# Another order of reading x in the first product of most first-layer blocks

## The chip, the core and the metric

The kernel runs on one core of one Trainium2 chip. The metric is the device time of one execution in microseconds (us); below, times before are the median of three runs. The engines named are TensorE (PE for its matrix products, PEld for its weight loads), VectorE (DVE), ScalarE (ACT), GpSimd (POOL) and the DMA queue of SyncE (SP, SPq). SBUF is the memory that the engines read their operands from, PSUM the one that TensorE writes its products to.

## The reference

A banded attention over 4 batches, 8 heads, 768 positions and 64 dimensions per head, and then a two-layer network on its output:

```python
scores = scale * np.matmul(q, k.transpose(0, 1, 3, 2))
keep = is_sink | in_window           # 4 sink positions, or the last 128
scores = np.where(keep, scores, -1000000000.0)
a = softmax(scores)                  # over the last axis
attn_out = np.matmul(a, v)           # 4 x 8 x 768 x 64
x = attn_out.transpose(0, 2, 1, 3).reshape(3072, 512)
h = x @ w_in                         # 512 x 2048
g = h - np.tanh(h)
out = g @ w_out                      # 2048 x 512
```

## The kernel before

The 3072 rows of x are worked on in 12 chunks of 256 positions. For each chunk and each pair of heads the kernel computes scores (tile `s`), softmax (`p`), transposes of it (`t`, `pt`) and the product with the values, which is x of the chunk, transposed: 128 partitions by 4 parts by 256 positions. It is kept as a rounded high part `xh` and the rest, `xl`. So are the weights of both layers (`w`) and the hidden values (`gh`, `gl`): a product of two such numbers is made of three products, high by high, high by low and low by high.

The network is worked on in 96 steps: a chunk `cc` with one of 8 groups `g` of 256 hidden columns. A step `n` has three parts:

- The first-layer block (`first_half`, `mm1`): 24 products of 256 columns into the PSUM tile `h`, two halves `f` of 128 hidden columns with 12 products each (4 parts `d` of x by the three combinations). The stationary operand is a 128x128 piece of the weights, loaded anew for each product, and the moving operand is the 256 columns of `xh` or `xl` of a part. These are the products of L721. Product `k` 0 is the first of them: `xh`, part 0, first half.
- The gate (`gate`): tanh on ACT (L726), h minus it on DVE (L729), the high part on ACT (L733), the low part on DVE (L737).
- The second-layer block (`second_half`, `mm2`): 12 products of 512 columns into the PSUM tile `o` (L769), eight with `gh`, then four with `gl` as stationary operand.

The blocks and the attention are handed to a planner (`Work`) as work items with an engine, a duration, a due time and the tiles that they read and write; `Work.order` simulates the engines and gives one list, and the instructions are then issued in this order on each engine. After an `o` block `rank` prefers a ready `h` block, and a block that was begun is finished before another one is taken, where its items are ready. So PE runs `h` and `o` blocks in turns, with attention products (`s`, `t`, `x`) between them or within them; at four places two `h` blocks stand one behind the other. The gate of step n runs on ACT and DVE while PE runs the `o` block of step n - 1 and the `h` block of step n + 1.

Of the kernel before, what the change touches and what calls it, by code (L numbers as in the profile page):

```python
# [42 lines left out]
def kernel(  # L43
# [50 lines left out]
    with tc.If(bad == 0) as cmp:  # L94
        _banded(tc, qd, kp, vp, vs, masks, w_in, w_out, ident, pts, early, out)
# [79 lines left out]
        _decode_part(nc, m.bitcast(U32), lo, hi, i)  # L175


FREE = 23


class Work:
# [28 lines left out]
    def order(self):  # L210
# [14 lines left out]
        def rank(n):  # L225

            b, due = self.block[n], self.all[n][2]
            if last is None or last[1] < FREE or self.all[n][0] != "PE":
                return (1, due, n)
# [33 lines left out]
def _banded(tc, qd, kp, vp, vs, masks, w_in, w_out, ident, pts, early, out):  # L263
    nc = tc.nc
    et = mybir.EngineType
    with ExitStack() as ctx:

        def pool(name, bufs, **kw):
            return ctx.enter_context(tc.tile_pool(name=name, bufs=bufs, **kw))
# [7 lines left out]
        spool, pp, sm = pool("spool", 1), pool("pp", 2), pool("sm", 4)  # L277
        ps_s, ps_t, ps_x = pool("ps_s", 1, space=PSUM), pool("ps_t", 1, space=PSUM), pool("ps_x", 1, space=PSUM)
        ps_h, ps_o = pool("ps_h", 2, space=PSUM), pool("ps_o", 1, space=PSUM)
        work = Work()  # L280


        RAW, TWO, CUT, DUO, PB, ZL, TK = 12, 12, 1, 3, 4, 0, 1100
# [427 lines left out]
        hps, gr, gh, gl, ops, ob = ({} for _ in range(6))  # L711

        def mm1(n, k):
            cc, g = order[n]
            if k == 0:
                hps[n] = ps_h.tile([P, 2, CH], F32, tag="h", name=f"h{n}")
            f, r = divmod(k, 12)
            d, t = divmod(r, 3)
            w = wt[0, g][:, (0, 0, 1)[t], d, f * P : (f + 1) * P]
            x = (xh, xl, xh)[t][cc][:, d, :]  # L720
            nc.tensor.matmul(hps[n][:, f, :], lhsT=w, rhs=x, start=r == 0, stop=r == 11)  # L721

        def gate(n):
            def tanh():
# [63 lines left out]
        def first_half(n):  # L788
            cc, g = order[n]
            for f in range(2):  # L790
                for z in range(2):
                    def some(k0=f * 12 + z * 6):
                        for k in range(k0, k0 + 6):
                            mm1(n, k)

                    x = [("xu", home(cc), 2 * z), ("xu", home(cc), 2 * z + 1), ("x", home(cc))]
                    work.add("PE", 722, due_step(n), some, x + [("w", 0, g)], [("h", n % 2)], block=("h", n))
# [67 lines left out]
        second_half(NS - 1)  # L865

        todo, _ = work.order()
        with tc.manual_schedule(engines={et.PE, et.SP, et.DVE, et.Activation, et.Pool}):
            for n in todo:
                work.all[n][3]()  # L870
# [204 lines left out]
```

## Time and profile before

| | us |
|---|---|
| median of three runs | 686.13 (685.95 to 686.75) |
| the profiled execution | 685.93 |
| its span, first to last instruction | 684.2 |
| PE busy in it | 670.8 (98%), 4604 products |
| DVE busy | 426.7 (62%) |
| ACT busy | 368.0 (54%) |

The span is what the trace covers; the execution's own time is 1.7 us longer. A product's record in the trace runs from its start to the modelled end of its last result, some 280 ns for 256 columns, and the records of products that follow each other overlap. How fast PE works is read from the distance between two starts. [...]

### The profile page before, as it was taken

What the parts mean: (1) busy time and instruction counts of PE and PEld (TensorE: products, weight loads), DVE (VectorE), ACT (ScalarE), POOL (GpSimd) and SP (SyncE); (2) the same over time, 40 slices, a digit from 0 to 9 for tenths busy, and PEclk for the clock granted to TensorE, in tenths of its full rate; (3) what the DMA queues carried; (4) which work ended last, traced back from release to release, by engine and by line L of the source; (5) the groups of instructions that cost most, each with busy time, mean ns of one, the idle gap of its engine ahead of it and who ended that gap; (6) DMA issues with size and microseconds to landing.
All of it is one profiled execution on the core that took longest, in us unless ns stands there. A gap on an engine that the chain in (4) does not pass through costs nothing.

```text
span 684.2 us, 12421 instructions
## 1 busy us (share of the span) xinstructions
PE 670.8 (98%) x4604; PEld 599.9 (88%) x4604; DVE 426.7 (62%) x1084; ACT 368.0 (54%) x1001; POOL 50.8 (7%) x201
## 2 busy tenths in 40 slices
PE   7999999999999999999999999999999999999997
PEld 5777899999989989989989998998998998998996
DVE  6889999937945656556655665565555656564221
ACT  5996433347835564465455655555556456553222
POOL 6220000000000010000001000001000000000000
PEclk9999999999999999999999999999999999999999
DMA  6789800022221122112103102012103101100001
GB/s 200 249 265 386 327 1 5 0 70 75 55 90 29 28 97 67 28 59 74 41 28 109 54 30 89 29 54 91 28 29 101 42 28 59 59 1 1 32 1 35
DMA packets 31713, 52.13 MB, mean 76 GB/s; under 512 B 3229, under 2 KB 21021, under 8 KB 31645
## 3 DMA queue, kind: packets, MB, share of 16 engines
q1 hardware_dynamic: 31340, 50.93, 22.8%
q8 instruction: 38, 0.62, 0.4%
q10 hardware_dynamic: 304, 0.33, 0.2%
q14 instruction: 31, 0.25, 0.1%
HBM read 44.96 MB, written 6.29 MB: 75 GB/s over the span
## 4 chain that ended last, share of the span: by engine, by line
PE 90%; ACT 4%; DVE 3%; SPq 1%; issue 1%; DMA 0%; POOL 0%; DVEq 0%; POOLq 0%; ACTq 0%
PE h L721 38%; PE o L769 38%; PE s L517 5%; PE x L650 5%; PE t L596 2%; ACT p L569 1%; ACT p L543 1%; PE x L644 1%; DVE pt L610 1%; DVE pt L169 1%; DMA qk<-kp 0%; DVE pt L167 0%; PE x L627 0%; DVE p L535 0%; SPq L106 0%
## 5 line engine op out<-in xcount | busy, mean ns | idle before, releaser
L721 PE MATMUL h<-xh,w 128*128 128x256 f32 x1536 | 287.1, 281 | 0.0
L721 PEld LDWEIGHTS h<-xh,w 128*128 128x128 f32 x1536 | 241.1, 188 | 3.3
L721 PE MATMUL h<-xl,w 128*128 128x256 f32 x768 | 215.5, 281 | 0.0
L769 PE MATMUL o<-w,gh 128*128 128x512 f32 x768 | 194.1, 393 | 0.6 <-ACT gh L733 0.6
L769 PEld LDWEIGHTS o<-w,gh 128*128 128x128 f32 x768 | 137.4, 188 | 26.0 <-ACT gh L733 1.0
L721 PEld LDWEIGHTS h<-xl,w 128*128 128x128 f32 x768 | 146.7, 191 | 3.2
L726 ACT ACTIVATE graw<-h 128x512 f32<-128x512 f32 x96 | 57.3, 596 | 165.1 <-PE h L721 164.8
L769 PE MATMUL o<-w,gl 128*128 128x512 f32 x384 | 103.6, 390 | 0.0
L543 ACT ACTIVATE p<-p,st 128x132 f32<-128x132 f32 x192 | 76.1, 399 | 48.4 <-DVE st L535 48.0
L737 DVE TENSOR_TENSOR gl<-h,gh 128x512 fp32r<-128x512 f32 x96 | 66.2, 690 | 46.7 <-ACT gh L733 46.4
L729 DVE TENSOR_TENSOR h<-h,graw 128x512 f32<-128x512 f32 x96 | 66.9, 696 | 42.3 <-ACT graw L726 41.4
L529 DVE COPY_PREDICATED s<-above,s 128x256 f32<-128x256 uint32 x80 | 33.9, 423 | 95.2 <-PE s L517 95.0
L769 PEld LDWEIGHTS o<-w,gl 128*128 128x128 f32 x384 | 71.7, 188 | 14.9
L733 ACT CAST gh<-h 128x512 fp32r<-128x512 f32 x96 | 56.2, 585 | 30.1 <-DVE h L729 30.0
L569 ACT ACTIVATE p<-p,st 128x132 f32<-128x132 f32 x192 | 62.1, 397 | 7.3 <-DVE st L564 7.1
L535 DVE CUSTOM_DVE_ANT_0 p<-s,mask 128x132 f32<-128x132 f32 x192 | 48.9, 292 | 8.1 <-POOL qraw L368 2.3
L517 PE MATMUL s<-ks,q 128*128 128x260 f32 x288 | 49.7, 294 | 0.0
L610 DVE TENSOR_TENSOR pt<-t,below 128x512 f32<-128x512 f32 (+1 forms) x48 | 28.8, 601 | 32.2 <-PE t L596 30.9
L574 POOL CAST z<-p 128x16 fp32r<-128x16 f32 x48 | 10.1, 211 | 506.4 <-ACT p L569 504.5
L479 DVE TENSOR_TENSOR ks<-kraw,ks 64x392 fp32r<-64x392 f32 x72 | 40.5, 562 | 5.7 <-ACT ks L474 3.5
L650 PE MATMUL x<-pt,v 128*64 128x128 f32 (+1 forms) x512 | 41.5, 315 | 0.0
L517 PEld LDWEIGHTS s<-ks,q 128*128 128x128 f32 x288 | 39.4, 189 | 2.0 <-issue 0.9
(77 smaller groups left out, 538.9 us busy)
## 6 DMA issues: line engine op xcount, KB each, us to landing
qraw<-qd SPq DMA_DIRECT2D x36, 256.0 KB, 2.8
wraw<-w_in SPq DMA_DIRECT2D x16, 512.0 KB, 7.0
wraw<-w_out SPq DMA_DIRECT2D x16, 512.0 KB, 7.9
kraw<-kp SPq DMA_DIRECT2D x37, 196.0 KB, 2.5
v<-vp SPq DMA_DIRECT2D x27, 256.0 KB, 2.8
out<-ob SPq DMA_DIRECT2D x24, 256.0 KB, 2.4
qk<-kp SPq DMA_DIRECT2D x8, 196.0 KB, 5.4
qk<-qd SPq DMA_DIRECT2D x16, 64.0 KB, 5.0
```

Of the source, the lines that this page charges most:

```text
L479: nc.vector.tensor_tensor(k[o, h, :], t[r, :], k[r, h, :].bitcast(F32), op=ALU.subtract)
L517: nc.tensor.matmul(ps[h][:, :WIN], lhsT=q[:, h, t * P : (t + 1) * P], rhs=rhs, start=i == 0, stop=i == 1,)
L535: nc.vector.tensor_tensor_reduce(out=pr[u][:, j, :], in0=ps[h][:, P:WIN], in1=mask[:, kind, :], scale=-0.125, scalar=BIG, op0=ALU.add, op1 ...
L543: nc.scalar.activation(e, e, AF.Exp, bias=st[u][:, j : j + 1], scale=-1.0, accum_out=st[u][:, 4 + j : 5 + j],)
L569: nc.scalar.activation(pr[u][:, j, :], pr[u][:, j, :], AF.Copy, scale=s[:, 8 + j : 9 + j])
L650: nc.tensor.matmul(xps[key][(p - p0) // 2][h * 64 : h * 64 + 64, p % 2, a:z], lhsT=vt[cc, i][:, hd : hd + D], rhs=rhs, start=False, stop=p ...
L721: nc.tensor.matmul(hps[n][:, f, :], lhsT=w, rhs=x, start=r == 0, stop=r == 11)
L726: nc.scalar.activation(gr[n], hps[n], AF.Tanh)
L729: nc.vector.tensor_tensor(hps[n], hps[n], gr[n], op=ALU.subtract)
L733: nc.scalar.copy(gh[n], hps[n])
L737: nc.vector.tensor_tensor(gl[n], hps[n], gh[n].bitcast(F32), op=ALU.subtract)
L769: nc.tensor.matmul(ops[cc, t], lhsT=(gh, gh, gl)[i][n][:, f, t * P : (t + 1) * P], rhs=wt[1, g][:, (0, 1, 0)[i], f, :], start=first and no ...
```

## The change

The first product (`k == 0`) of an `h` block now reads its 256 columns of `xh`, and writes its 256 columns of `h`, in another order, if the PE work item that is issued ahead of the block's first item is not one of an `h` block. The 256 columns are taken as four quarters (`b`) of four pieces (`k`) of 16 columns (`l`, 64 bytes); the rearranged view runs over the pieces first and the quarters within: piece 0 of the four quarters, then piece 1 of the four, and so on. Both sides have the same view, so each column is multiplied and written to the same place as before. The weights, the other 23 products of the block and all else stay as they are. `before` records for each block what the list from the planner has ahead of it; the planner itself is given the same items and durations.

```diff
+def _pieces(t, parts, size, back=False):
+    v = t.rearrange("p (b k l) -> p k b l", b=parts, l=size)
+    return v[:, ::-1] if back else v
...
-        work = Work()
+        work, before = Work(), {}
...
             x = (xh, xl, xh)[t][cc][:, d, :]
-            nc.tensor.matmul(hps[n][:, f, :], lhsT=w, rhs=x, start=r == 0, stop=r == 11)
+            y = hps[n][:, f, :]
+            if k == 0 and before["h", n] != "h":
+                x, y = (_pieces(a, 4, 16) for a in (x, y))
+            nc.tensor.matmul(y, lhsT=w, rhs=x, start=r == 0, stop=r == 11)
...
         todo, _ = work.order()
+        came = None
+        for n in todo:
+            if work.all[n][0] == "PE":
+                b = work.block[n]
+                if b:
+                    before.setdefault(b, came)
+                came = b and b[0]
```

In the built programs the order is the same on all five engines; 92 products of PE, one in each of 92 of the 96 `h` blocks, have another form. One of them, on PE, behind the last `o` block (`o`) of a chunk and its attention, where the `h` block of the next chunk begins; before:

```order
L769 MATMUL o_6723<-w_7_1708,gh_7124 128x512 x8
L769 MATMUL o_6723<-w_7_1708,gl_7155 128x512 x4
L721 MATMUL h_7177<-xh_7161,w_0_578 128x256
L721 MATMUL h_7177<-xl_7162,w_0_578 128x256
L721 MATMUL h_7177<-xh_7161,w_0_578 128x256 x2
L721 MATMUL h_7177<-xl_7162,w_0_578 128x256
```

The same place on PE in the changed program (L721 is now L730, L769 is L778):

```order
L778 MATMUL o_6723<-w_7_1708,gh_7124 128x512 x8
L778 MATMUL o_6723<-w_7_1708,gl_7155 128x512 x4
L730 MATMUL h_7177<-xh_7161,w_0_578 128x4x4x16
L730 MATMUL h_7177<-xl_7162,w_0_578 128x256
L730 MATMUL h_7177<-xh_7161,w_0_578 128x256 x2
L730 MATMUL h_7177<-xl_7162,w_0_578 128x256
```

Nothing has moved; the first product of the block has 4 by 4 by 16 columns in place of 256.

## Rows read from the trace of the kernel before

**Rows 1.** The page: busy time and instructions of each engine, and TensorE's granted clock.

```profile
PE 670.8 (98%) x4604; PEld 599.9 (88%) x4604; DVE 426.7 (62%) x1084; ACT 368.0 (54%) x1001; POOL 50.8 (7%) x201
...
PEclk9999999999999999999999999999999999999999
```

**Rows 2.** The page's chain that ended last, shares of the span by engine.

```profile
PE 90%; ACT 4%; DVE 3%; SPq 1%; issue 1%; DMA 0%; POOL 0%; DVEq 0%; POOLq 0%; ACTq 0%
```

**Rows 3.** The chain in time (start, length, what), 70 to 690 us: blocks of PE.

```profile
73.87 2.83 PE h L721 x24
76.69 2.75 PE o L769 x12
79.44 2.83 PE h L721 x24
...
196.82 2.76 PE h L721 x24
...
253.75 5.66 PE h L721 x48
...
670.85 2.83 PE h L721 x24
```

**Rows 4.** The chain in time, 150 to 182 us.

```profile
156.19 0.48 PE s L517 x4
156.67 1.86 PE o L769 x8
158.53 2.72 PE h L721 x24
...
164.48 0.93 PE o L769 x4
165.41 2.72 PE h L721 x24
...
171.89 0.47 PE o L769 x2
172.35 2.74 PE h L721 x24
...
178.80 0.49 PE s L517 x4
179.29 2.83 PE h L721 x24
```

**Rows 5.** PE's instructions in time (start, length, what), a block of 24 products.

```profile
140.58 0.28 PE L721 MATMUL h<-xh,w 128*128 128x256 f32 x1
140.70 0.28 PE L721 MATMUL h<-xl,w 128*128 128x256 f32 x1
...
143.41 1.32 PE L769 MATMUL o<-w,gh 128*128 128x512 f32 x5
```

**Rows 6.** The same, another block of 24 products.

```profile
158.36 0.28 PE L721 MATMUL h<-xh,w 128*128 128x256 f32 x1
...
161.08 0.28 PE L517 MATMUL s<-ks,q 128*128 128x260 f32 x1
```

**Rows 7.** Weight loads in time, the second one of the block of rows 5.

```profile
140.59 0.19 PEld L721 LDWEIGHTS h<-xl,w 128*128 128x128 f32 x1
```

**Rows 8.** PE's instructions in time, scores in plain f32 and the begin of an early block.

```profile
32.87 1.04 PE L510 MATMUL s<-qk 128*128 128x260 f32 x4
33.75 0.38 PE L627 MATMUL x<-ident,z 128*128 128x128 f32 x2
33.88 0.37 PE L721 MATMUL h<-xh,w 128*128 128x256 f32 x1
34.08 0.28 PE L721 MATMUL h<-xl,w 128*128 128x256 f32 x1
```

**Rows 9.** ACT in time, the high part of the gate behind rows 5.

```profile
145.03 0.59 ACT L733 CAST gh<-h 128x512 fp32r<-128x512 f32 x1 [0.77 <-DVE h L729]
```

**Rows 10.** PE in time, the first products that use it.

```profile
148.98 2.00 PE L769 MATMUL o<-w,gh 128*128 128x512 f32 x8
```

## The prediction, made before the changed kernel was run

> **What bounds the kernel now.** I read the busy times first: PE is busy for 98% of the span and has the full clock in every slice [rows 1]. The chain that ended last is PE for 90% [rows 2], so a nanosecond on PE is nearly always a nanosecond of the kernel. Then I followed that chain in order of time [rows 3]: from 73.87 us on it is `h` blocks of 24 products and `o` blocks of 12, one behind the other, 2.83 and 2.75 us long, with no piece of another engine between. No wait is there to be removed; what can change is how long PE's own products take.
>
> The next view was the same chain where its order is less regular [rows 4]. The reader is to see there that the same block of 24 products has two lengths: 2.83 us and 2.72 us, with two between (2.74 here, and one of 2.76 at 196.82 [rows 3]). Single starts tell the same. In the block at 140.58 the first `o` product starts 2.83 us later, 118 ns for each product [rows 5]; in the block at 158.36 the next work on PE starts 2.72 us later, 113 ns for each [rows 6]. Clock, shapes, tiles and number of products are equal. So `h` products run at one of two paces 4.6 ns apart, and a block keeps its pace. Counted in that chain over the whole span, 77 single blocks take 2.83 us (the first and the last are in [rows 3]), four pairs take 5.66 us, which is twice 2.83 (one is in [rows 3]), one block of two halves has the slow pace too, and four blocks are faster. The rest lies in the start, before 74 us.
>
> What decides the pace shows in what ran ahead. Behind a full `o` block of 12 the pace is slow each time [rows 3]. The three faster blocks of [rows 4] follow `o` products that were cut by scores into pieces of 8, 4 and 2. Behind a piece of four scores the pace is slow again (179.29). And the second block of a pair takes over the pace of the first. So what carries the pace is a relation in time between the streams, set at the block's begin and kept: the load of the next weights starts 10 ns behind the product that it lies under [rows 5, 7], and the two read SBUF together all through the block. That the two reads are what locks is my reading; the two paces and their dependence on the begin are the rows'.
>
> [...]
>
> **The change part by part.** It adds and removes no instruction, wait or transfer, and the order of all engines is the same. It changes the moving read and the PSUM write of one product in each of 92 blocks.
>
> *First term, the pace of the other 23.* If the new first product moves the two streams against each other as the cut `o` blocks do, the block runs at the fast pace. The blocks that are slow now and begin with a changed product are 77 single ones, four pairs (their second block takes over the pace) and the split one: 77 x 0.11 + 4 x 0.22 + half of 0.11 = 8.47 + 0.88 + 0.06 = 9.4 us. The first product itself is not at the new pace: 82 begins x 0.11 / 24 = 0.4 us less. That leaves 9.0 us.
>
> *Second term, the changed product itself and what it takes to settle.* No row has a moving operand in pieces. [...] From above: the slowest rate of such a width here is that of the plain f32 scores, four starts in 33.75 - 32.87 = 0.88 us, 0.22 us each [rows 8], 0.11 more than a fast `h` product: 92 x 0.11 = 10.1 us. The first `h` product at 33.88 also holds the next one up for 0.20 us [rows 8], 0.09 over the pace, but it starts beside a transposition that is still running. The nearest rows are the blocks that begin out of step and then settle: 2.74 and 2.76 against 2.72 [rows 3, 4], 0.02 to 0.04 us. I take 0.03: 92 x 0.03 = 2.8 us.
>
> *What comes late next.* With the steps 0.11 us shorter, the gate has less time. Now the high part is ready at 145.03 + 0.59 = 145.62 us [rows 9] and PE first uses it at 148.98 [rows 10]: 3.36 us of cover against 0.2 us that two blocks lose. DVE and ACT, at 62% and 54% [rows 1], have room for 1%. I give nothing back here.
>
> *The sum* against the profiled execution: 685.93 - 9.0 + 2.8 = 679.7 us. The median of the runs shown is 0.2 us above that execution, so 679.9; I forecast 680.0 us.
>
> **The rivals.**
>
> *The pace stays (686.1 us).* A 64-byte piece may be just what is fetched at a time anyway. Then the new order changes addresses but not timing, the first product takes as long as ever, and the streams keep their relation. For it: blocks that begin behind four scores stay slow too, as the one at 179.29 [rows 4], so not every other begin frees a block. Against it: all three begins behind cut `o` products did. [...]
>
> *The pieces cost and free nothing (slower).* Place: the changed product alone. Price: between nothing and 0.11 us for each; it decides from 1.4 us / 92 = 15 ns on. The 64-byte jumps in SBUF or in PSUM would stretch that product to some pace between 0.12 and 0.22 us, and the next 23 would fall back into the slow pace as they do behind scores. At half of the bound, 0.05 us, the time is 686.1 + 4.6 = 690.7; at the whole of it 696.2. Against it: the same columns in the same number are read and written, and runs of 16 columns are long.
>
> [...]
>
> *The pieces cost much and free the block all the same.* With 0.11 us each, 686.1 - 9.0 + 10.1 = 687.2 us: no difference that can be told.
>
> *Only a part is freed.* If about half the begins, say those behind uncut `o` blocks at one of the phases, go over to the fast pace, 4.5 us are gained and 2.8 paid: 684.4 us.
>
> **How the numbers follow.** The whole forecast gets 0.51: the paces are there, and of the begins that differ from a full `o` block, those behind cut `o` products went fast and those behind scores did not; a begin with a product of another form is a third kind, and nearer to the first, since the same `o` products lie ahead. A part freed: 0.07. The pace stays: 0.16, and much paid for all that is gained: 0.05. Pieces that cost and free nothing: 0.21. About 0.2%, 1.4 us, is what a measurement of this kernel can tell from no change. So faster 0.51 + 0.07 = 0.58, the same 0.16 + 0.05 = 0.21, slower 0.21. The likeliest case's own range is 676.7 (all of the 9.4 us, nothing paid) to 683 (0.06 us paid for each). The range that holds 8 in 10 goes from 676.7 over the unmoved 686.1 to 688.7, which is the third case with a price of 0.028 us; above it lies about half of that case and little else.
>
> **What would show it.** In the chain in time, `h` blocks of 24 at 2.72 to 2.76 us in place of 2.83, and pairs at some 5.45 to 5.50; the start of the second product of a block, now 0.12 us behind the first [rows 5], shows the price of the changed one. `o` blocks should stay at 2.75 us, since they begin alike behind fast and slow `h` blocks. The forecast is wrong if the `h` blocks still read 2.83 (the pace stays) or more (the pieces cost), or if the second starts lie over 0.2 us behind the first ones.

## The result, and the profile after

The changed kernel takes 679.9 us (679.37 to 680.06) beside 686.13 for the kernel before in the same series: a ratio of 0.9905, 95% interval 0.9891 to 0.992. Its profiled span is 678.3 us where it was 684.2; PE is busy for 98% of it as before, and the granted clock is full in every slice (0.999 over the span), as in [rows 1]. Of all the runs behind this text one was slow: it took 1113.62 us at a granted clock of 0.555, with the kernel that takes the pieces backwards, and is left out below; the others had 0.997 to 1.0.

The first view to compare is the chain in order of time (start, length, what) with [rows 3]:

```profile
74.14 2.74 PE h L730 x24
76.88 2.74 PE o L778 x12
79.62 2.74 PE h L730 x24
...
252.24 5.47 PE h L730 x48
...
664.64 2.74 PE h L730 x24
```

The chain has the same pieces in the same order. An `h` block of 24 is now 2.74 us long where it was 2.83, a pair 5.47 where it was 5.66, and the `o` blocks here keep their length to 0.01. Counted over the whole chain, 82 single blocks take 2.73 to 2.76 us and one takes 2.82; before, 79 took 2.83 and four were faster. The prediction's count of 77 left two out.

The second view is one block, product by product, to be read against [rows 5] (start, length, what):

```profile
139.82 0.28 PE L730 MATMUL h<-xh,w 128*128 128x256 f32 x1
139.93 0.28 PE L730 MATMUL h<-xl,w 128*128 128x256 f32 x1
140.05 0.40 PE L730 MATMUL h<-xh,w 128*128 128x256 f32 x2
140.29 0.28 PE L730 MATMUL h<-xl,w 128*128 128x256 f32 x1
...
142.56 0.63 PE L778 MATMUL o<-w,gh 128*128 128x512 f32 x2
```

The reordered product holds the next one up for 0.11 us, no longer than a plain one did. The first four products take 140.29 - 139.82 = 0.47 us, 118 ns each, which is the slow pace; the other 20 take 142.56 - 140.29 = 2.27 us, 113 ns each, which is the fast one of [rows 6]. Over the 76 blocks of 24 that follow an `o` block, the distances of the starts are on average 117, 117, 122, 119 and then 113.3 ns; before they were 117 to 118 from the first product to the last.

**Where the 5.9 us of span come from.** The 83 single blocks of the chain go from a mean of 2.824 to 2.745 us: 6.5. Four pairs: 4 x 0.19 = 0.8. Against that some `o` blocks behind scores became longer. Before and after, in the chain in time:

```profile
436.39 0.48 PE s L517 x4
436.87 2.76 PE o L769 x12
...
442.45 0.48 PE s L517 x4
442.93 2.73 PE o L769 x12
445.67 2.83 PE h L721 x24
```

```profile
432.81 0.49 PE s L523 x4
433.30 2.74 PE o L778 x12
...
438.78 0.47 PE s L523 x4
439.25 2.77 PE o L778 x12
442.02 2.75 PE h L730 x24
```

Where scores alone stand between an `h` block and the `o` block, this went from 2.73 to 2.77 (24 blocks). Where transposes stand ahead of the scores, as at 436.39, it went from 2.76 to 2.74 (19 blocks). The mean of the 84 whole ones rose from 2.745 to 2.754, which costs 0.8 us. So the blocks gave 6.5 + 0.8 - 0.8 = 6.5 us, and smaller pieces 0.1.

Of these 6.6 us 0.7 are lost again, at the two ends of the span. The first `h` block of the chain's regular part starts at 74.14 us against 73.87 [rows 3], behind a stretch in which PE waits for DVE and ACT. From the end of the last copy of the output to the end of the span it is 4.8 us against 4.4. Both ends differ from run to run: in the kernel below that changes the read alone the regular part starts at 73.72, and over all kernels of this text the stretch behind the last copy takes 4.4 to 5.2 us. So neither is put down to the change.

### The profile page after: what moved, and what is told of

It reads as the page before. It is cut to its first block, busy times and chain, and to the rows that moved or that the text cites. A ratio compares the mean times of both kernels' runs of the same rounds, so it can differ in the third digit from the quotient of the medians.

```text
span 678.3 us, 12421 instructions
## 1 busy us (share of the span) xinstructions
PE 664.6 (98%) x4604; PEld 592.8 (87%) x4604; DVE 426.7 (63%) x1084; ACT 368.0 (54%) x1001; POOL 51.1 (8%) x201
## 4 chain that ended last, share of the span: by engine, by line
PE 90%; ACT 3%; DVE 3%; SPq 1%; issue 1%; POOL 1%; DMA 1%; POOLq 0%; ACTq 0%
PE o L778 39%; PE h L730 37%; PE s L523 5%; PE x L656 5%; PE t L602 2%; ACT p L575 1%; ACT p L549 1%; PE x L650 1%; DMA qk<-kp 1%; DVE p L541 0%; DVE pt L167 0%; PE x L633 0%; DVE pt L169 0%; SPq L106 0%; DVE pt L616 0%
## 5 line engine op out<-in xcount | busy, mean ns | idle before, releaser
L730 PE MATMUL h<-xh,w 128*128 128x256 f32 x1536 | 279.9, 278 | 0.0
L730 PEld LDWEIGHTS h<-xh,w 128*128 128x128 f32 x1536 | 239.1, 188 | 3.3
L730 PE MATMUL h<-xl,w 128*128 128x256 f32 x768 | 212.5, 277 | 0.0
L778 PE MATMUL o<-w,gh 128*128 128x512 f32 x768 | 194.6, 394 | 0.6 <-ACT gh L742 0.6
L778 PEld LDWEIGHTS o<-w,gh 128*128 128x128 f32 x768 | 137.2, 188 | 26.4 <-ACT gh L742 1.0
L730 PEld LDWEIGHTS h<-xl,w 128*128 128x128 f32 x768 | 144.2, 188 | 3.2
L778 PE MATMUL o<-w,gl 128*128 128x512 f32 x384 | 103.9, 391 | 0.0
L778 PEld LDWEIGHTS o<-w,gl 128*128 128x128 f32 x384 | 71.7, 188 | 15.4
L656 PEld LDWEIGHTS x<-pt,v 128*64 128x64 f32 x512 | 31.0, 137 | 11.7 <-issue 4.8
```

The lines of the kernel that those rows point to most:

```text
L656: nc.tensor.matmul(xps[key][(p - p0) // 2][h * 64 : h * 64 + 64, p % 2, a:z], lhsT=vt[cc, i][:, hd : hd + D], rhs=rhs, start=False, stop=p ...
L730: nc.tensor.matmul(y, lhsT=w, rhs=x, start=r == 0, stop=r == 11)
L778: nc.tensor.matmul(ops[cc, t], lhsT=(gh, gh, gl)[i][n][:, f, t * P : (t + 1) * P], rhs=wt[1, g][:, (0, 1, 0)[i], f, :], start=first and no ...
```

## The experiments

The theory: the stream of x and the loads of the weights meet in SBUF in a relation that is set at the block's begin and kept, a slow one or a fast one, and the changed product puts the block on the way to the fast one. Each ratio is to the kernel before in the same series. Parts of an edit that are not shown are marked with three points.

**Is it the read or the write?** Two kernels each have one side of the change alone, so the first product of 92 blocks lands in wrong columns; the work stays the same.

```diff
-                x, y = (_pieces(a, 4, 16) for a in (x, y))
+                x, y = _pieces(x, 4, 16), y.rearrange("p (k b l) -> p k b l", b=4, l=16)
```

> Only the read of x is in pieces; the 256 columns are written to PSUM in plain order, so the first product of 92 blocks lands in wrong columns. Theory (the order of the reads shifts the stream of x against the weight loads and frees the block from the slow pace): as the changed kernel, 679.9 us within 0.7, blocks of 24 at 2.74. Rival (the PSUM write in pieces does it): 686.1 us, blocks at 2.83.

```diff
-                x, y = (_pieces(a, 4, 16) for a in (x, y))
+                x, y = x.rearrange("p (k b l) -> p k b l", b=4, l=16), _pieces(y, 4, 16)
```

> Only the PSUM write is in pieces, x is read in plain order, so the first product of 92 blocks lands in wrong columns. Theory (reads): 686.1 us, blocks of 24 at 2.83, second product still 0.12 us behind the first. Rival (the write does it): 679.9 us. [...]

Measured: the read alone 679.59 us, ratio 0.9904 (0.9888 to 0.9921); the write alone 686.22, ratio 1.0002 (0.9992 to 1.0012). Chain in time, first the read alone, then the write alone:

```profile
134.07 2.74 PE h L730 x24
```

```profile
135.26 2.83 PE h L730 x24
```

The read of x does all of it. The write in 64-byte pieces costs nothing that these runs can tell, so the rival that had the pieces cost in PSUM has no price. Runs of 16 f32 values cost nothing here (686.22 us with and without them).

**Does the place in the block matter?** The same reordered product as product 12.

```diff
-            if k == 0 and before["h", n] != "h":
+            if k == 12 and before["h", n] != "h":
```

> The same reordered product, but product 12 of the block instead of product 0 (same 92 blocks). Theory (a relation between two streams, kept until something shifts it): products 0 to 11 at 118 ns, some four to settle, the rest at 113; a block of 24 takes 2.80 us; 82 begins times (12 x 4.4 - 22 ns) = 2.5 us gained, 683.6. Rival (it is the switch from 512 to 256 columns that sets the pace, and only there it can be changed): 686.1, blocks at 2.83.

Measured: 686.79 us, ratio 1.0006 (0.9996 to 1.0015). The 683.6 of the theory did not come, and the rival's time did. PE's instructions in time, products 0, 11 with 12, and the end (start, length, what):

```profile
140.47 0.28 PE L730 MATMUL h<-xh,w 128*128 128x256 f32 x1
...
141.77 0.40 PE L730 MATMUL h<-xh,w 128*128 128x256 f32 x2
...
143.30 0.40 PE L778 MATMUL o<-w,gh 128*128 128x512 f32 x1
```

The whole block takes 143.30 - 140.47 = 2.83 us. But the product does move something: over 76 blocks the distances from product 12 on are 119, 114.5, 118, 118 and then 117 to 118 again, with 121 before the next block. So the theory needs a correction: it is not enough to disturb the relation. The slow pace drew this disturbance back. Why the same product works at the begin is open: before the change the first distance of such a block is 118 ns already, so no row shows that the slow relation is not yet there. 74 single blocks in the chain read 2.83.

The other nine are faster, and they show two things more. One of them, in the chain in time, is the block that read 2.83 at 179.29 in [rows 4]:

```profile
179.24 2.77 PE h L730 x24
```

Its distances are 113 to 114 ns from its fourth product on, before its reordered product comes, and so are those of four others that begin behind four scores as it does and read 2.83 before. So the pace of those blocks was changed by something ahead of their own first product; what it is was not followed. And in these fast blocks the product in the middle makes the distances 117, 122, 119, 124, 118 and then 113 to 114 again: the fast pace draws the disturbance back as the slow one does.

**Must it be a product on x?** The `h` blocks as before the change, and the last product of each `o` block reads (and writes) its 512 columns in pieces (`_pieces` as in the change).

```diff
+            x, y = wt[1, g][:, (0, 1, 0)[i], f, :], ops[cc, t]
+            if k == 11:
+                x, y = (_pieces(a, 8, 16) for a in (x, y))
...
-                ops[cc, t], lhsT=(gh, gh, gl)[i][n][:, f, t * P : (t + 1) * P],
-                rhs=wt[1, g][:, (0, 1, 0)[i], f, :],
+                y, lhsT=(gh, gh, gl)[i][n][:, f, t * P : (t + 1) * P],
+                rhs=x,
```

> The h blocks are as before the change; in place of them the last product of each of the 96 o blocks reads its 512 columns (and writes them) in 64-byte pieces of eight parts in rotation. Theory (any shift of the moving stream shortly ahead frees the h block): blocks of 24 at 2.72 to 2.76, 678 to 681 us. Rival (only a product of the h block itself, on x, can do it): 686.1, blocks at 2.83.

Measured: 679.52 us, ratio 0.99 (0.9883 to 0.9916). Chain in time:

```profile
134.20 2.74 PE h L727 x24
```

So no product of the `h` block has to be touched: a shift just ahead of it is as good. It does on purpose what the `o` blocks cut by scores did in [rows 4], though not in the same way: there the fast pace holds from the first product (in the blocks at 158.53 and 165.41), here the first three take 120, 124 and 118 ns.

**Do other orders do it?** Pieces of 256 bytes, and the same 64-byte pieces backwards.

```diff
-                x, y = (_pieces(a, 4, 16) for a in (x, y))
+                x, y = (_pieces(a, 2, 64) for a in (x, y))
```

> The changed kernel with other pieces: two halves of two pieces of 64 columns (256 bytes) in turns, so the first product reads its quarters in the order 0, 2, 1, 3. Theory (any shift of the read of x at this place frees the block): blocks of 24 at 2.74 to 2.76, 679 to 682 us. Rival (only jumps at every 64 bytes do): 2.83 us, 686.1.

```diff
-                x, y = (_pieces(a, 4, 16) for a in (x, y))
+                x, y = (_pieces(a, 4, 16, True) for a in (x, y))
```

> The changed kernel with the same pieces in reverse: piece 3 of the four quarters first, piece 0 last. Theory (the block needs to be moved off its first relation, and the number of products to settle depends on where it is put): fast pace at the end, blocks of 24 at 2.72 to 2.76 us, 677.5 to 682 us. Rival (the one order tried is special): 2.83 us, 686.1.

Measured: 256-byte pieces 686.44 us, ratio 1.0 (0.999 to 1.0009); backwards 679.64, ratio 0.9897 (0.9877 to 0.9917). Chain in time, the large pieces, then the small ones backwards:

```profile
135.32 2.83 PE h L730 x24
```

```profile
134.18 2.74 PE h L730 x24
```

The theory's "any shift" falls a second time: a change of order every 256 bytes leaves the block where it was, a change every 64 bytes frees it, forwards or backwards. With the larger pieces the number of jumps is smaller too (3 for 15), so size and number are not told apart; sizes between were not tried.

**What does reading in pieces cost when all products do it?**

```diff
-            if k == 0 and before["h", n] != "h":
+            if True:
```

> All 24 products of every h block read x and write h in 64-byte pieces of the four quarters. Theory (two streams of equal stride lock at a slow or a fast relation): jumps at every 64 bytes break up the lock, each product takes 113 to 117 ns, blocks of 24 at 2.72 to 2.80 us, 677 to 684 us. Rival (the piece read itself costs and is worth it only once a block): over 118 ns each, above 686.1.

Measured: 691.63 us, ratio 1.007 (1.0054 to 1.0087). Chain in time:

```profile
135.68 2.87 PE h L730 x24
```

2.87 us are 120 ns for each product, 6 ns over the fast pace, as the rival had it. Whether the pieces themselves cost this, or a third relation between the streams, is not shown: 120 ns is also the pace of a kernel below without any pieces. Either way pieces in every product are no better way to read; they pay only as a single push.

**Is it the address of x against that of the weights?** Three kernels without any piece read move tiles in SBUF: x 64 bytes up, all of them 64 bytes down (the tile `gap`, of 16 columns, is left out), and the weights 64 down with x 64 up. Where x moves, the hidden values move with it.

```diff
+        pool("gap2", 1).tile([P, 16], F32, tag="gap2", name="gap2")
         qpool, vpool, hpool = pool("qpool", 2), pool("vpool", 3), pool("hpool", 1)
```

> The kernel before, with x, the hidden values and what lies behind them in SBUF 64 bytes higher, the weights where they were. Theory A (the two streams meet at an address relation, so a shift of 64 bytes acts like a shift in time): h blocks of 24 leave 2.83 us, to 2.72 to 2.76 or to another length at least 0.02 away; 677 to 682 us if fast. Theory B (only the relation in time counts): 2.83 us, 686.1.

```diff
-        pool("gap", 1).tile([P, GAP], F32, tag="gap", name="gap")
```

> The kernel before without its first 64-byte tile (gap), so weights, x and all behind lie 64 bytes lower together. Theory (the address of x against that of the weights sets the pace): nothing changes, h blocks of 24 at 2.83, o blocks at 2.75, 686.1 us within 1. Rival (each address by itself, or its place in the memory's rows, counts): blocks away from 2.83 by 0.02 or more, as when x alone was 64 bytes higher (2.87, 696.2 us).

```diff
-        pool("gap", 1).tile([P, GAP], F32, tag="gap", name="gap")
...
+        pool("gap2", 1).tile([P, 32], F32, tag="gap2", name="gap2")
```

> The kernel before with the weights 64 bytes lower and x and what lies behind it 64 bytes higher: x is 128 bytes further from the weights than before. Theory (the address of x against that of the weights): another relation, h blocks of 24 at a third length, 2.72 to 2.95 us; a guess that each 64 bytes cost one more slot gives 2.87 or more, 696 us or more. Rival (x at its absolute place): as with x alone 64 bytes higher, 2.87 and 2.81, 696.2 us.

Measured: x up by 64 bytes 696.17 us, ratio 1.0136 (1.0119 to 1.0153); all down 686.63, ratio 0.9999 (0.999 to 1.0009); x up by 128 against the weights 690.78, ratio 1.0061 (1.0044 to 1.0078). Chain in time, in this order:

```profile
131.59 2.87 PE h L722 x24
134.46 2.81 PE o L770 x12
```

```profile
135.11 2.83 PE h L720 x24
137.94 2.75 PE o L768 x12
```

```profile
129.90 2.83 PE h L721 x24
132.73 2.78 PE o L769 x12
```

Moved together, nothing changes. Moved against each other, both kinds of block change, and by different amounts: `o` blocks, in which the stationary operand is one of the moved tiles, go from 2.75 to 2.81 and 2.78; `h` blocks to 2.87 and, with 128 bytes, back to 2.83. x has the same absolute address in the first and the third, yet the lengths differ. The weights have the same in the second and the third, and the `o` blocks differ there. So neither address alone accounts for the lengths, while their relation accounts for all four kernels. My guess of a fixed cost for each 64 bytes is wrong. And 10 us lie in where a tile begins: the same program took 686 or 696 us.

**Does the load take part?** Products 1 to 10 of each 12 with 64 stationary columns.

```diff
-            nc.tensor.matmul(hps[n][:, f, :], lhsT=w, rhs=x, start=r == 0, stop=r == 11)
+            m = 64 if 0 < r < 11 else P
+            nc.tensor.matmul(hps[n][:m, f, :], lhsT=w[:, :m], rhs=x, start=r == 0, stop=r == 11)
```

> The kernel before with 64 in place of 128 stationary columns in products 1 to 10 of each 12 of an h block, so half of the hidden columns lack ten of their twelve products. Theory (the slow pace is the weight load's read against the read of x): with half the load the 4.4 ns over the fast pace shrink to 2.2 or to nothing, blocks of 24 at 2.72 to 2.78 us, 677 to 682 us. Rival (the load has no part in it): 2.83 us, 686.1.

Measured: 683.92 us, ratio 0.9962 (0.9947 to 0.9976). PE's instructions in time, a block of 24 (the shorter loads read 128*64):

```profile
139.94 0.28 PE L722 MATMUL h<-xh,w 128*128 128x256 f32 x1
140.06 0.28 PE L722 MATMUL h<-xl,w 128*64 128x256 f32 x1
...
141.25 0.40 PE L722 MATMUL h<-xh,w 128*128 128x256 f32 x2
141.48 0.28 PE L722 MATMUL h<-xl,w 128*64 128x256 f32 x1
...
142.73 0.63 PE L770 MATMUL o<-w,gh 128*128 128x512 f32 x2
```

From product 0 to 11 it is 141.25 - 139.94 = 1.31 us, 119 ns each; from there on 142.73 - 141.25 = 1.48 us for 13, 114 ns each. The time, 683.92 us, lies between those of the theory and of the rival. x, the clock and the 256 columns of each product are the same, so either the shorter load or what comes with it takes part: a product with 64 stationary columns also writes half of the partitions of `h`, and the two were not tried apart. Half of the load does not halve the 4.4 ns, as the theory had it. The first half of the block is as slow as ever, and behind the two full loads in its middle the second half is fast, with loads of the same length as in the first. So the length of the load does not set the pace by itself; there are two paces again, and a block went from one to the other at a change in the sequence.

**Can the settling of the `o` block be had too?** The changed kernel with the first `o` product in pieces.

```diff
+            x, y = wt[1, g][:, (0, 1, 0)[i], f, :], ops[cc, t]
+            if k == 0:
+                x, y = (_pieces(a, 8, 16) for a in (x, y))
...
-                ops[cc, t], lhsT=(gh, gh, gl)[i][n][:, f, t * P : (t + 1) * P],
-                rhs=wt[1, g][:, (0, 1, 0)[i], f, :],
+                y, lhsT=(gh, gh, gl)[i][n][:, f, t * P : (t + 1) * P],
+                rhs=x,
```

> The changed kernel, and the first product of each of the 96 o blocks reads its 512 columns in 64-byte pieces of eight parts in rotation too. The first five products of an o block behind an h block take 27 ns more than five later ones. Theory (that is the same kind of settling, begun at another relation): the settling changes, blocks of 12 between 2.72 and 2.77 us, 677.5 to 681.5 us. Rival (it is the end of the h block's loads, whatever the order): 2.75 us, 679.9.

Measured: 679.61 us, ratio 0.9899 (0.9882 to 0.9915), not to be told from the changed kernel; chain in time:

```profile
131.64 2.75 PE o L781 x12
134.40 2.74 PE h L730 x24
```

The `o` blocks settle by another way and in nearly the same time: the mean of the 84 whole ones is 2.749 us, against 2.754 in the changed kernel, 0.4 us in all. None of the 12 kernels is faster than the changed one by more than the runs scatter.

## Why the prediction was right

**What bounds the kernel**, PE's own pace with no wait to remove: right; the gain is in the length of single blocks, and from 74.14 us to the end of the last `o` block the chain is PE alone, with the same pieces as before.

**The first term**, slow blocks that go over to the fast pace: right in kind, and in number but for two. I counted 82 begins where there are 84, 79 single blocks and not 77. All but the block at 185.51, which still reads 2.82, and the second half of the split block are freed, and the second blocks of pairs follow the first ones, as forecast (5.47). The reading behind it, that a relation of two reads carries the pace, is supported by the tiles that were moved together and against each other, and by the read and the write taken apart. That the streams lock in SBUF is still a reading. 64 bytes between x and the weights made an `h` product 2.87 / 24 = 120 ns long where it takes 113 at best.

**The second term**, 0.03 us for each begin: measured are 21 ns in the first four products and 2 ns before the `o` block, so 0.023. The source was not the one that the bound stands for: the product in pieces takes 117 ns and is not slow; products 2 and 3, plain ones, are. The upper bound of 0.11 us from the plain f32 scores had nothing to do with it; the rows of blocks that settle were the right neighbours. But those lengths, 2.74 and 2.76, hold the first product already, so the 0.4 us that the first term takes off for it were counted twice. The two terms together gave 6.2 us; 6.5 + 0.8 = 7.3 came. The 1.1 us between are the 0.4, some 0.2 for the two blocks left out, and 0.5 for begins that cost 23 ns and not 30.

**What comes late next**, nothing given back: wrong by 0.8 us. The gate did keep its cover, since PE alone is in the chain. But the `o` blocks behind scores have their own settling, and its length depends on what ran ahead. I had read only those behind `h` blocks, of which I wrote that they would stay at 2.75 us, and those did. That the total came out at 679.9 is so in part by luck: the gain in the `h` blocks was put too low by 1.1 us and the loss in the `o` blocks, 0.8, was not seen.

**The rivals.** That the pace stays is refuted for this order, but it is what 256-byte pieces do (686.44 us), so the chance that I gave it was not idle. What I named for it, the blocks behind scores that stay slow, was a weak sign: five of the six whole blocks that begin so are now fast. That their own changed product did it is not shown, since five of them are fast too where only product 12 was changed. That the pieces cost is refuted for one product in 24; with all 24 the kernel is slower (691.63 us), for whichever reason.

**What stays open.** Why a block of the kernel before keeps one of two paces, 118 ns or 113, why a push at the begin moves a block and one in the middle does not, and why jumps every 64 bytes do it and jumps every 256 do not. The trace has no record of single reads.

## What to carry to other kernels

Where PE is busy all the time and no wait is left, compare the lengths of equal blocks in the chain: two lengths of the same block at the same clock are a term of their own, and its price is their difference times the count. What ran ahead of the shorter blocks tells what might free the longer; then a push at the begin can be tried, in the `h` block or just ahead of it (679.9 and 679.52 us here), while one in the middle of a block (686.79 us) was drawn back to the pace that the block had, slow or fast. And before any rearranging of work, move one operand's tile by 64 bytes against the other: here that alone was worth 10 us to the worse.

## What the runs showed of the hardware that was not expected

Products of 256 columns took 113.3 ns on average from start to start once a block of the changed kernel had settled, 117.6 in the slow blocks of the kernel before (117.8 in its pairs), and 2.87 / 24 = 120 ns with x 64 bytes further from the weights. Those of 512 columns took 226.7 ns from the sixth to the eleventh of an `o` block behind an `h` block, before the change and after it, and on average 2.81 / 12 = 234 ns in the `o` blocks of the kernel with x 64 bytes up. All of this is at the same granted clock (0.997 to 1.0); what differed was the address of x or of the hidden values against the weights, and what ran ahead. In the kernels before and after, the settled pace of an `h` block lasted to its last product or the one ahead of it, in pairs through 48 products (117.8 and 113.3 ns). With shorter loads it changed within the block, from 119 ns to 114, and a reordered product in the middle moved it for some four or five products only (119, 114.5, 118 and 118 ns, then 117 to 118 again).
